# Three of the second round's low weight parts: GpSimd subtraction in place of an adding transfer

## The chip, the cores and the metric

One core of one Trainium2 chip runs the whole kernel. The metric is device time in microseconds (us) of one execution; a profiled execution gives, beside it, a trace of every engine. The engines are TensorE (PE; its weight loads PEld), VectorE (DVE), ScalarE (ACT), GpSimd (POOL) and SyncE (SP, which here only starts transfers and reads one index).

## The reference

Windowed attention is followed by a layer of eight experts. Attention: `q`, `k`, `v` are (8, 8, 576, 64); half of the heads look 32 positions back, half look at every fourth of the last 128; softmax, then times `v`. The result, as `x` of 4608 tokens by 512, goes to the experts:

```
logits = x @ w_gate                      # 4608 x 8
# tokens go to experts in the order of their logits, at most 576 to each
h = maximum(x[mask] @ w1[e], 0.0)        # w1[e]: 512 x 1024
out[mask] = h @ w2[e]                    # w2[e]: 1024 x 512
```

All is float32. Which expert fills up first, and with which tokens, depends on the data, so the kernel finds it by a search, once a round.

## The kernel before

Attention fills the first 205 us or so; the rest is `moe` (from L1110), eight rounds of one expert each. The change lies in round two, which the code counts as `r == 1`.

**A round.** A search on DVE and PE (counting matmuls, L782, between DVE steps, L796 and L819 to L832) finds the expert. `settle` and `listing` make its list of 576 tokens: `digits` on DVE, the products `rx` on POOL (`by_chunk`, L1079) and ACT, six comparisons `ob` on DVE (`within`, L1087), 18 placing matmuls (`place`, L1094), then `indices` on DVE (L1103 to L1106). Five indirect transfers on POOL (`gather`, L1258) fetch the tokens; PE turns them (L1272), and ACT and DVE split them into a high part `xh` and a low part `xl` (through one PSUM tile, so one after the other). GEMM 1 (L1309) multiplies by `w1`, GEMM 2 (L1351) by `w2`; results go out by an indirect transfer on POOL (`put`, L1377, behind a small memset, L1376) from a ring of three `y` tiles.

**Weights.** Full precision comes from two reduced parts of each float32 weight: a high one `h`, rounded by ACT, and a low one `l = raw - h`. `weights(n, r, f, deps)` (L1143) loads piece `f` of eight (128 x 512) of `w1` or `w2` (L1159, started by SP), makes `h` on ACT (`hi`, L1164, seen in the trace at the helper's line L1141), and then `l` in one of two ways. Where `(n, r)` is in `ADDED`, which holds `("2", 0)`, `("1", 1)` and `("2", 1)`, ACT writes `-h` into `l` (`ne`, L1167) and POOL starts a transfer that adds `raw` to it (L1169). Elsewhere DVE subtracts (L1171, in the trace at L1142). In round two only the first four pieces of `w1` are loaded as soon as the expert is known; the other four wait for a gate, a tiny POOL memset (L1150).

**The order of the work.** Each engine runs its instructions in the order in which they were issued, and that order is made while the program is built, by a planner (`Schedule.run`). Every piece of work has an engine, a price in ns, the pieces it needs and a boost; its due time is the length of what follows it, less the boost. On each engine the piece with the earliest due time goes next, from when it is ready; another piece goes ahead of one that is not ready yet only if it ends, by its price, at most a tolerance later than that one could start. For POOL the tolerance `TOL_POOL` is 200 ns. Some prices: `by_chunk` 750, each `within` 473, `close` (DVE) 1780, `place` 450, `indices` 620, each `get` of the gather 1250, `put` 1200, and 180 from engine to engine; the boosts are 27000 for a gather, 23000 for the list, 1500 for weights and -15000 for a `put`. In round two POOL runs, in this order: `put` of the first y tile, `rx`, the adding transfers of pieces 0, 1 and 2, `put` of the second y tile, five gathers, the gate, the adding transfer of piece 3, `put` of the third.

Of the kernel before, what the change touches and what calls it, by code (L numbers as in the profile page):

```python
# [38 lines left out]
B_L, B_G, B_T, B_X, B_H, B_HL, B_Y, B_S, B_W = 23000, 27000, 15000, 0, 20000, 17000, 28000, -15000, 1500  # L39
RAW1, D_R, NQ, AHEAD_W = 8, 262, (2, 2), (3, 4)  # L40
ADDED, T_A, T_G = (("2", 0), ("1", 1), ("2", 1)), 4500, 4500
# [114 lines left out]
class Schedule:  # L156
# [8 lines left out]
    def op(self, eng, cost, fn, deps=(), boost=0, lat=0, dma=0, buf=None):  # L165
        x = Op(len(self.ops), eng, cost, fn, deps, boost, lat, dma, buf)
        for d in x.deps:
            d.users.append(x)
        self.ops.append(x)
        return x  # L170
# [940 lines left out]
def moe(tc, ctx, C, R, xd, w1, w2, out):  # L1111
    nc = tc.nc
# [7 lines left out]
    op = K.op  # L1120
# [21 lines left out]
    sub = lambda e, o, a, b: e.tensor_tensor(o, a, b, op=OP.subtract)  # L1142
    E, gemm1_end, x_users, got, gate = {}, {}, {}, {}, {}  # L1143

    def weights(n, r, f, deps):

        raw, old, use = RAW[n].take()
        if n == "1" and r < len(AHEAD_W) and f == AHEAD_W[r]:

            gate[r] = op("POOL", 100, lambda: nc.gpsimd.memset(raw[:1, :1], 0.0), [got[r, 1], *old], B_G)  # L1150
        if r in gate:
            deps = [*deps, gate[r]]

        def load():
            if n == "1":
                src = w1[bass.ds(E[r], 1), f].rearrange("o p d f -> p (o d f)")
            else:
                src = w2[bass.ds(E[r], 1), f * 128:f * 128 + 128, :].rearrange("o p d -> p (o d)")
            nc.sync.dma_start(raw, src)  # L1159

        ld = op("SP", 60, load, [*deps, *old], dma=T_W)
        h, oldh, useh = WH[n].take()
        l, oldl, usel = WL[n].take()
        hi = op("ACT", 525, lambda: act(h, raw), [ld, *oldh], B_W)  # L1164
        if (n, r) in ADDED:
            use.append(hi)
            ne = op("ACT", 525, lambda: nc.scalar.activation(l, h.bitcast(F32), AF.Copy, scale=-1.0), [hi, *oldl], B_W)  # L1167
            useh.append(ne)
            lo = op("POOL", 1040, lambda: nc.gpsimd.dma_start(l, raw, accum_op=OP.add), [ne], B_W, lat=T_A)  # L1169
            use.append(lo)  # L1170
        else:  # L1171
            lo = op("DVE", 600, lambda: sub(nc.vector, l, raw, h), [ld, hi, *oldl], B_W)
            use += [hi, lo]
        useh.append(lo)
        return h, l, hi, lo, useh, usel
# [216 lines left out]
    def round_(r):  # L1392
        e = None
        if r:
            e = search(r) if r < NE - 1 else chain("DVE", 650, R.last, [st["fetch"], st["need"]])
        en = st["fetch"] = EN[r] = op("SP", 100, lambda: fetch(r, R.eidx), [e])
        ix, BOX[r] = settle(r, e)
        X[r] = gather(r, ix, BOX[r])
        W[r] = [weights("1", r, f, [en]) for f in range(NF)]

    round_(0)
    for r in range(NE):
        W2 = [weights("2", r, f, [EN[r]]) for f in range(NF)]
        expert(r, X[r], BOX[r], W[r], W2)
        if r + 1 < NE:
            round_(r + 1)
# [78 lines left out]
```

## Time and profile before

| what | us |
|---|---|
| median of three executions | 704.34 (703.73 to 706.86) |
| the profiled execution, its own time | 708.44 |
| its span, first to last instruction | 706.6 |

The median is of runs without a profile. Every row below comes from the one profiled execution, which took 4.10 us longer than that median, and whose span lies 1.84 us under its own time. Times in rows are us from the start of the span. A busy PE is not PE at its peak, since the ends of matmuls are modelled; spans on POOL are rough.

### The profile page before, as it was taken

Reading aid. Unit: us, or ns where it says so; the run is one execution under the profiler, and the core shown is the slowest. Engines: PE = TensorE matmul, PEld = TensorE weight load, DVE = VectorE, ACT = ScalarE, POOL = GpSimd, SP = SyncE. Lnnn points to the kernel's source line nnn. Section 1 sums busy time; section 2 is a strip of 40 time slices with the busy share of each in tenths; the row PEclk is TensorE's granted clock in tenths of the full one; section 3 lists DMA queues with packets and bytes.
Section 4 is the critical chain, followed back from the end, with each engine's and each line's share of the span. In section 5 each row is a group of like instructions: output and inputs, shape, how many; then the busy total and the mean of one; then the engine's idle time right before and its main releaser. Section 6 shows DMA issues by size and latency. Waiting matters only on the chain.

```text
span 706.6 us, 17388 instructions
## 1 busy us (share of the span) xinstructions
PE 665.0 (94%) x6579; PEld 585.0 (83%) x6581; DVE 484.7 (69%) x2086; ACT 291.4 (41%) x616; POOL 140.6 (20%) x206
## 2 busy tenths in 40 slices
PE   7899999999974899899999999999999999999995
PEld 5787899888963698699889889879978988988983
DVE  5467877789457889588689879969978854724200
ACT  3344554453521474286335434423524525424210
POOL 6111111100000332452410410310321131211011
PEclk9999999999985899999999999999999999999998
DMA  9999999973211684889314514512711574113001
GB/s 253 266 265 284 279 311 255 264 202 80 63 41 45 194 177 112 249 174 268 98 53 137 180 51 130 185 43 73 239 51 53 164 261 147 50 58 98 1 23 45
DMA packets 58524, 104.60 MB, mean 148 GB/s; under 512 B 6212, under 2 KB 27844, under 8 KB 58436
## 3 DMA queue, kind: packets, MB, share of 16 engines
q1 hardware_dynamic: 49096, 78.32, 38.7%
q0 software_dynamic: 9344, 25.17, 13.4%
q8 instruction: 51, 0.84, 0.5%
q14 instruction: 33, 0.27, 0.1%
HBM read 78.31 MB, written 18.87 MB: 138 GB/s over the span
## 4 chain that ended last, share of the span: by engine, by line
PE 68%; issue 12%; DVE 10%; POOL 3%; DMA 3%; ACT 1%; another core or an unknown queue 1%; POOLq 0%; SPq 0%; DVEq 0%
PE py L1351 18%; PE ph L1309 17%; PE pS L506 9%; PE px L514 6%; PE px L564 3%; PE pS L503 3%; PE pm L486 2%; PE ptx L1272 2%; PE pz L782 2%; PE py L1354 1%; PE py L1356 1%; POOL out L1377 1%; DVE hb L1329 1%; DVE G L796 1%; DMA qs<-in_qd 1%
## 5 line engine op out<-in xcount | busy, mean ns | idle before, releaser
L1351 PE MATMUL py<-w2h,hb 128*128 128x512 f32 x512 | 172.0, 401 | 0.0
L1309 PE MATMUL ph<-xh,w1h 128*128 128x256 f32 (+1 forms) x512 | 138.1, 300 | 0.0
L1309 PE MATMUL ph<-xl,w1h 128*128 128x256 f32 (+1 forms) x512 | 136.8, 298 | 0.0
L1309 PE MATMUL ph<-xh,w1l 128*128 128x256 f32 (+1 forms) x512 | 136.0, 296 | 0.0
L1351 PEld LDWEIGHTS py<-w2h,hb 128*128 128x128 f32 x512 | 96.7, 189 | 19.4
L1351 PE MATMUL py<-w2l,hb 128*128 128x512 f32 x256 | 100.2, 392 | 0.0
L1141 ACT ACTIVATE hb<-ph 128x256 fp32r<-128x256 f32 (+2 forms) x192 | 59.6, 345 | 88.5 <-PE ph L1309 86.9
L1309 PEld LDWEIGHTS ph<-xh,w1h 128*128 128x128 f32 x512 | 91.8, 190 | 0.5
L1309 PEld LDWEIGHTS ph<-xh,w1l 128*128 128x128 f32 x512 | 91.8, 190 | 0.1
L1309 PEld LDWEIGHTS ph<-xl,w1h 128*128 128x128 f32 x512 | 91.4, 190 | 0.1
L506 PE MATMUL pS<-q,k 128*80 128x96 f32 (+1 forms) x672 | 83.0, 265 | 0.0
L1377 POOL DMA_INDIRECT out<-y,idx x40 | 41.3, 1034 | 194.6 <-ACT y L1141 136.0
L456 ACT ACTIVATE E<-pS 96x384 f32<-96x384 f32 (+1 forms) x96 | 46.5, 486 | 75.2 <-PE pS L506 74.1
L1329 DVE SCALAR_TENSOR_TENSOR hb<-ph,hb 128x320 fp32r<-128x320 f32 (+1 forms) x128 | 57.0, 452 | 29.4 <-ACT hb L1141 25.2
L506 PEld LDWEIGHTS pS<-q,k 128*80 128x80 f32 (+1 forms) x672 | 68.5, 158 | 0.0
L1141 ACT ACTIVATE y<-py 128x512 f32<-128x512 f32 (+1 forms) x40 | 23.8, 596 | 104.0 <-PE py L1351 90.5
L493 DVE CUSTOM_DVE_ANT_0 junkm<-pm,const 128x80 bf16<-128x80 f32 (+1 forms) x336 | 59.5, 244 | 4.2 <-PE pm L486 3.6
L1351 PEld LDWEIGHTS py<-w2l,hb 128*128 128x128 f32 x256 | 48.6, 190 | 8.5
L514 PE MATMUL px<-v,E 81*64 81x65 f32 (+1 forms) x1344 | 47.9, 225 | 5.3 <-issue 2.9
L1258 POOL DMA_INDIRECT xg<-xd,idx x40 | 42.1, 1054 | 52.7 <-PE ph L1309 25.1
L514 PEld LDWEIGHTS px<-v,E 81*64 81x64 f32 (+1 forms) x1344 | 42.8, 138 | 10.2 <-issue 3.8
L1141 ACT ACTIVATE w1h<-raw 128x512 fp32r<-128x512 f32 x64 | 39.6, 628 | 27.6 <-DMA raw<-in_moe_w 27.2
(179 smaller groups left out, 1009.5 us busy)
## 6 DMA issues: line engine op xcount, KB each, us to landing
raw<-in_moe_w SPq DMA_DIRECT2D x128, 256.0 KB, 4.6
v<-in_vp SPq DMA_DIRECT2D x8, 780.0 KB, 14.2
v<-in_vd SPq DMA_DIRECT2D x8, 650.0 KB, 10.3
xd<-xs SPq DMA_DIRECT2D x16, 288.0 KB, 7.5
xd<-xs SPq DMA_DIRECT2D x32, 144.0 KB, 9.2
w2l<-raw POOLq DMA_DIRECT2D x16, 256.0 KB
qs<-in_qp SPq DMA_DIRECT2D x7, 576.0 KB, 10.1
k<-in_kp SPq DMA_DIRECT2D x7, 576.0 KB, 9.7
```

The lines of the kernel that those rows point to most:

```text
L456: e = self.op("ACT", 380, lambda j=j, pS=pS: nc.scalar.activation(self.E[:self.nk, j * self.gs:j * self.gs + self.gs], pS.tile[:, :self.gs ...
L493: nc.vector.tensor_tensor_reduce(out=jk[:, c - c0, :nk], in0=pm[:, (c - c0) * nk:(c - c0 + 1) * nk], in1=mm[:, min(1, (c if self.kind == 0 ...
L503: nc.tensor.matmul(pS[:nk, c - c0], ls[:64 + n, c], self.r[:64 + n, :2 * nq], start=(c == c0), stop=False, skip_group_check=True)
L506: nc.tensor.matmul(pS[:nk, c - c0], self.Ks[c], self.Qm[c], start=False, stop=True, skip_group_check=True)
L514: nc.tensor.matmul(px[64 * a:64 * a + 64, c - c0], lh, self.V[c][a], start=True, stop=True)
L564: nc.tensor.transpose(t[:, c], src, C["identf"])
L1141: act = lambda o, i, f=AF.Copy: nc.scalar.activation(o, i, f)
L1258: nc.gpsimd.indirect_dma_start(out=xg[:n], out_offset=None, in_=xd, in_offset=bass.IndirectOffsetOnAxis(ap=box[0][:n, m:m + 1], axis=0))
L1309: nc.tensor.matmul(o, a[:, d * 128:d * 128 + 128], b[:, d, c0:c1], start=((d, i) == pairs[0]), stop=((d, i) == pairs[-1]))
L1329: hl = op("DVE", 335 if j == 0 else 400, lambda: nc.vector.scalar_tensor_tensor(hb[:, CAP + c0:CAP + c1], o, 0.0, hb[:, c0:c1], op0=OP.max ...
L1351: nc.tensor.matmul(py, x, w, start=(f + i == 0), stop=(f == NF - 1 and i == 2))
L1377: s = nc.gpsimd.indirect_dma_start(out=out, out_offset=bass.IndirectOffsetOnAxis(ap=box[0][:n, m:m + 1], axis=0), in_=y[:n], in_offset=None)
```

## The change

For round two's `w1` (`n == "1"`, `r == 1`) and pieces 0, 1 and 2, the negated copy on ACT and the adding transfer are gone. In their place POOL subtracts, `l = raw - h`, at a price of 1900 ns, once the load and the high part are there. Pieces 3 to 7 of the same round keep the adding transfer.

```
         hi = op("ACT", 525, lambda: act(h, raw), [ld, *oldh], B_W)
-        if (n, r) in ADDED:
+        if (n, r) == ("1", 1) and f < 3:
+
+            lo = op("POOL", 1900, lambda: sub(nc.gpsimd, l, raw, h), [ld, hi, *oldl], B_W)
+            use += [hi, lo]
+        elif (n, r) in ADDED:
             use.append(hi)
             ne = op("ACT", 525, lambda: nc.scalar.activation(l, h.bitcast(F32), AF.Copy, scale=-1.0), [hi, *oldl], B_W)
             useh.append(ne)
```

`sub(e, o, a, b)` is `e.tensor_tensor(o, a, b, op=OP.subtract)`. The adding transfer that these pieces leave carried a price of 1040 and 4500 ns (`T_A`) until it lands.

## Rows read from the trace of the kernel before

**Rows 1.** From the page: the span, and the busy time of each engine with its share and its number of instructions.
```profile
span 706.6 us, 17388 instructions
...
PE 665.0 (94%) x6579; PEld 585.0 (83%) x6581; DVE 484.7 (69%) x2086; ACT 291.4 (41%) x616; POOL 140.6 (20%) x206
```

**Rows 2.** The chain of work that ended last, from 276 to 286.5 us (start, length, what).
```profile
276.00 5.47 PE py L1351 x24
281.47 0.47 PE ptx L1094 x18
281.93 4.22 PE py L1351 x18
286.15 0.56 PE pz L782 x9
```

**Rows 3.** Who waited for whom from 276 to 300 us: engine and instruction that waited, what released it, then total us, times, longest. "remote" is a release that the trace puts to no instruction.
```profile
ACT xh L1141 <- remote: 4.8, 1, 4.8
...
DVE Q L819 <- remote: 3.7, 1, 3.7
...
PE pz L782 <- DVE G L796: 2.7, 1, 2.7
...
PE ptx L1272 <- DVE xl L1142: 0.5, 1, 0.5
```

**Rows 4.** The same core by stretches: length, busy us and instructions (x) of PE, PEld, DVE, ACT and POOL, then the granted TensorE clock as a share of full speed, the DMA engines' busy share, GB/s.
```profile
292.00:294.80 2.80, 0.14 (x2) 0.07 (x2) 1.98 (x9) 0.60 (x1) 0.26 (x1) 1.00 1.03 245
294.80:298.50 3.70, 3.23 (x18) 2.71 (x18) 3.32 (x12) 1.12 (x2) 0.00 (x0) 0.54 1.04 384
```

**Rows 5.** GpSimd (POOL) in order of time, 277 to 291 us: start, length, engine, line, operation, names, and in brackets the idle time before it and what ended that.
```profile
277.62 1.04 POOL L1079 TENSOR_TENSOR rx<-oa,const 128x360 bf16<-128x360 bf16 x1 [0.75 <-DVE oa L1074]
278.61 0.88 POOL L1169 DMA_DIRECT2D w1l<-raw  x1
...
282.50 1.04 POOL L1377 DMA_INDIRECT out<-y,idx  x1 [0.28 <-issue]
283.84 1.03 POOL L1258 DMA_INDIRECT xg<-xd,idx  x1 [0.30 <-DVE A L1053]
...
289.86 0.09 POOL L1150 MEMSET raw<- 1x1 f32 x1
289.89 1.03 POOL L1169 DMA_DIRECT2D w1l<-raw  x1
```

**Rows 6.** ScalarE (ACT) in order of time, columns as in rows 5: the first round-two weight pieces, and the copy out of the round-one matmul result that comes last.
```profile
276.66 0.63 ACT L1141 ACTIVATE w1h<-raw 128x512 fp32r<-128x512 f32 x1 [1.13 <-DMA raw<-in_moe_w]
277.33 0.63 ACT L1167 ACTIVATE w1l<-w1h 128x512 fp32r<-128x512 f32 x1
...
278.35 0.62 ACT L1141 ACTIVATE w1h<-raw 128x512 fp32r<-128x512 f32 x1
...
303.60 0.59 ACT L1141 ACTIVATE y<-py 64x512 f32<-64x512 f32 x1
```

**Rows 7.** Grouped rows: line, engine, operation, names, shape, number | busy us, mean ns of one | idle before, and what ended it. GpSimd's issuing of the eight adding transfers into w1l, and VectorE's subtractions into w1l in the other rounds, both over the whole span; then VectorE's wider hb subtractions from 300 to 620 us.
```profile
L1169 POOL DMA_DIRECT2D w1l<-raw x8 | 7.5, 940 | 9.5 <-ACT w1h L1141 8.5 <-ACT w1l L1167 1.0
...
L1142 DVE TENSOR_TENSOR w1l<-raw,w1h 128x512 fp32r<-128x512 f32 x56 | 36.2, 684 | 0.1
...
L1329 DVE SCALAR_TENSOR_TENSOR hb<-ph,hb 128x320 fp32r<-128x320 f32 x48 | 23.3, 486 | 8.1 <-ACT hb L1141 4.8 <-issue 2.8
```

**Rows 8.** VectorE (DVE) against GpSimd, columns as in rows 5. The six ob instructions of round two together; its second and its fourth alone; then rx on GpSimd and the ob beside it in a later round; then rx on GpSimd and an hb subtraction, which reads PSUM, beside it.
```profile
277.45 3.50 DVE L1087 TENSOR_TENSOR ob<-si,const 128x384 bf16<-128x384 int32 x6
...
277.92 1.16 DVE L1087 TENSOR_TENSOR ob<-si,const 128x384 bf16<-128x384 int32 x1
...
279.47 0.55 DVE L1087 TENSOR_TENSOR ob<-si,const 128x384 bf16<-128x384 int32 x1
...
381.66 0.79 POOL L1079 TENSOR_TENSOR rx<-oa,const 128x360 bf16<-128x360 bf16 x1 [14.27 <-DVE oa L1074]
...
381.89 0.97 DVE L1087 TENSOR_TENSOR ob<-si,const 128x384 bf16<-128x384 int32 x1
...
326.84 0.79 POOL L1079 TENSOR_TENSOR rx<-oa,const 128x360 bf16<-128x360 bf16 x1 [2.51 <-DVE oa L1074]
...
327.03 0.49 DVE L1329 SCALAR_TENSOR_TENSOR hb<-ph,hb 128x320 fp32r<-128x320 f32 x1 [0.27 <-ACT hb L1141]
```

**Rows 9.** TensorE (PE) in order of time: the list's placing matmuls, the first count of the next search, and the first turn of a gathered tile.
```profile
281.31 0.62 PE L1094 MATMUL ptx<-rx,ob 128*128 128x40 bf16 x18
...
286.00 0.46 PE L782 MATMUL pz<-G,ohr 128*128 128x64 bf16 x9
...
289.41 0.63 PE L1272 MATMUL ptx<-const,xg 128*128 128x128 f32 x4
```

**Rows 10.** Stretches with idle TensorE and the ones behind them, columns as in rows 4.
```profile
18.40:20.70 2.30, 0.00 (x0) 0.00 (x0) 1.12 (x5) 1.06 (x2) 0.00 (x0) 1.00 1.01 204
...
22.00:25.40 3.40, 3.40 (x29) 3.24 (x26) 2.36 (x26) 0.49 (x1) 0.00 (x0) 0.50 1.04 383
...
58.60:59.90 1.30, 0.05 (x2) 0.05 (x2) 0.51 (x1) 0.00 (x0) 0.00 (x0) 1.00 1.02 357
...
59.90:63.00 3.10, 3.10 (x50) 2.88 (x50) 2.33 (x20) 0.55 (x2) 0.74 (x2) 1.00 1.04 387
```

## The prediction

> **What bounds the kernel now.** I read the page first. PE is busy 665.0 of 706.6 us and POOL 140.6 [rows 1], so a change on POOL matters only where it moves a wait of PE. Then the chain of waits around the change: from 276 to 286.5 us it is PE alone, back to back, with the placing matmuls of the token list and the first count of the next search among the GEMM's [rows 2]. So in this stretch nothing can be won by relieving ACT, POOL or the transfers, and whatever holds PE's next instruction is lost in full, because the later rounds are PE's too.
>
> The view of who waited for whom shows the one hole nearby: PE waits 2.7 us for VectorE's G and 0.5 for xl [rows 3]. Behind that wait stand VectorE and ACT, both held 3.7 and 4.8 us by a release that the trace puts to no instruction. The table by stages shows PE nearly empty from 292 to 294.8, then granted 0.54 of its clock for 3.7 us [rows 4], mostly the lower of its two levels, 1.2 GHz. The hole costs 2.7 + 0.5 + 3.7 x 0.46 = 4.9 us. The profiled execution took 708.44; without the hole it would have been 703.5, close to the median of the runs shown, 704.34, and to the fastest, 703.73. So I read the hole as belonging to this execution, not to the median, and say below what follows if that is wrong.
>
> **What is removed.** Three negated copies on ACT, 0.63 us each [rows 6]: 1.9 us of ACT, whose own wait there is for loads (1.13 us before the first w1h). Nothing on PE waits for them; I cost this at nothing, covered by PE's GEMM 2. Three issues on POOL at 0.94 [rows 7], 2.8 us, and three transfers. These could have delayed the gathers behind them on the same queue. But the first gathered tile, issued at 283.84 [rows 5], is turned by PE at 289.41 with no wait noted [rows 9]. So no gain is taken; its bounds are 0 and the whole hole, 4.9, should the transfers be what held VectorE and ACT.
>
> **What is added, and where the planner puts it.** By the prices in the code, rx ends 0.93 us after the list's digits; two subtractions at 1.90 end at 4.73. The indices are ready at 5.24 (six within at 0.473, close 1.78, indices 0.62) and the gathers can start at 5.42. A third subtraction would end at 6.63, past 5.42 plus the tolerance of 0.20. So subtractions 0 and 1 run between rx and the gathers. The second y tile's put, a 1.20 piece that may start only when its tile is copied, no longer fits either. Behind the gathers the gate and piece 3 come by due time, then subtraction 2, then the two puts. Moving that put by some 12 us costs nothing: its tile is next written at 303.60 [rows 6]. SP's loads for pieces 4 to 7 wait for the gate, a POOL memset that stays behind the five gathers and slides with them.
>
> **Price of a subtraction on POOL.** The trace has none of this kind. The nearest POOL row with two SBUF inputs is rx, 0.79 us for 360 columns where it does not wait [rows 8]; scaled to 512, 1.12. The low bound is VectorE's own subtraction of this shape, 0.684 [rows 7]; the high one is rx as it ran in round two, 1.04 [rows 5], scaled: 1.48. I take 1.12, because the engine and the kind of work are the same. GPSIMD Engine Reference in the Trainium skill (Engine selection) puts a two-input operation on GpSimd at about twice VectorE's time, which would be 1.37; the sum below would then be 0.5 us higher, an estimate by that page that nothing here needs.
>
> **What it blocks.** This is the step that decides. After rx, VectorE runs the list's six ob comparisons, 3.50 us in all, ending at 280.95; PE's placing matmuls start at 281.31 [rows 8, 9]. That is a margin of 0.36. An ob takes 0.55, but 1.16 beside rx in round two and 0.97 in a later round, where it ends 0.41 us after rx ends (382.86 against 382.45) [rows 8]. So VectorE does nothing of an ob while rx runs, and then does it whole. The first two high parts are ready early (276.66 + 0.63, and 278.35 + 0.62 [rows 6]), so subtractions 0 and 1 run directly behind rx, among the five ob that remain. VectorE loses both: 2 x 1.12 = 2.24 us. PE's stall is 2.24 - 0.36 = 1.9 us. With the bounds on the price it is 1.0 to 2.6; with all three ahead of the gathers it is 3.0. The rest of VectorE's work (the indices, G, the count that PE reaches at 286.00) slides by the same 2.2, as PE has by 1.9, so it is not paid twice; the gathers start about 2.2 later too, and their tiles keep their lead on PE.
>
> The third subtraction, near 293 to 295 us, meets a search step and the xl subtractions. Those read PSUM, and an hb subtraction of that kind took 0.49 beside rx [rows 8], against a mean of 0.486 [rows 7]. So only a step that reads two SBUF tiles can be held. Bounds 0 and 1.12; I take 0.3, near the low end because of the hb row. SBUF — State Buffer in the Trainium skill (Who interferes with whom) says the same split as a rule: a VectorE instruction with two SBUF inputs waits for the whole of a GpSimd instruction that reads SBUF, one with a single SBUF input not at all. The trace agrees (0.97 against 0.55 for ob, 0.49 against 0.486 for hb). Were it sharing instead, each subtraction would cost what rx cost the ob of round two, 0.61 us, scaled 0.87, and the stall would be 1.4 instead of 1.9.
>
> **The sum.** 1.9 + 0.3 = 2.2 us more. On the profiled execution's own time that is 710.6 with its hole, 705.7 without. On the median, which I take to have no hole, it is 704.34 + 2.2 = **706.5**.
>
> **Rivals.** First, slower: the stall lowers PE's clock. An idle stretch of 2.3 us in attention was followed by 3.4 us at half clock, one of 1.3 us by none [rows 10]; the forecast's 1.9 lies between. Half of 3.4 us is 1.7, giving 708.2. It decides at an idle time somewhere from 1.3 to 2.3 us. For it: the hole above also ended at the low clock [rows 4]. Against it: with the low price the stall is 1.0, under the stall that did nothing.
>
> Second, faster: the hole is in the timed runs as well, and the three transfers make it, since they run on the queue just ahead of it. Then 4.9 goes and 2.2 comes: 701.6; with the subtractions hidden, 699.4. For it: the hole follows the only stretch where adding transfers and gathers share a queue. Against it: the unexplained release, the first gather's timely landing, and 708.44 against 704.34.
>
> Third, nothing happens: subtractions wait behind the gathers, or POOL takes its turn only where VectorE reads one SBUF tile. Then nothing on PE moves and the time is 704.3. Against it: the prices place two of them ahead, and rx got its turn among the ob.
>
> **How the numbers follow.** About 0.5% (3.5 us) is what a measurement of this kernel can tell from no change; the bounds are 700.8 and 707.9. Forecast 0.45, with stalls of 1.0 to 3.0 plus 0 to 1.1: 705.3 to 708.4, a tenth of it over the bound. Clock 0.25, most of it over the bound. Nothing 0.14. Hole 0.16, half of it under 700.8. Slower 0.04 + 0.22 = 0.26, faster 0.08, same 0.66. The range reaches from 701.5, which takes in the hole with the subtractions paid, to 709.0, which takes in the clock with a stall somewhat longer than forecast; what it leaves out is half of the hole's chance and the tail of the clock's.
>
> **What the profile after would show.** Right: two POOL subtractions of 1.0 to 1.5 us between rx and the first gather; two of the ob at 1.5 us or more, or one near 2.8; PE idle close to 2 us ahead of the placing matmuls, put to VectorE; the first gather 2 us later against the list's digits. Wrong: PE without a gap there (then VectorE was not held, or the planner put the work elsewhere); a subtraction of 1.9 us or longer, which makes the stall 3.4; a hole near 292 that is gone from timed runs too, told by a median near 701; a granted clock of 0.5 behind the stall, which is the first rival.

## The result

Twelve executions of each kernel: a median of 709.21 us (705.20 to 715.17) after, 704.28 (701.14 to 708.93) before; ratio 1.0076, 95% interval 1.0051 to 1.0101, which is 3.6 to 7.1 us more. A second series of the changed kernel, of six executions, gave 1.0100 (1.0070 to 1.0129). The forecast was 706.5, 2.2 us more than before, in a range from 701.5 to 709.0. The sign was the forecast's; the median lies 2.7 us above the forecast and 0.2 above the range, and the stages below account for 6.1 us instead of 2.2.

### The profile page after: what moved, and what is told of

It reads as the page before. It is cut to its first block, busy times and chain, and to the rows that moved or that the text cites. A ratio compares the mean times of both kernels' runs of the same rounds, so it can differ in the third digit from the quotient of the medians.

```text
span 711.3 us, 17384 instructions
## 1 busy us (share of the span) xinstructions
PE 666.4 (94%) x6581; PEld 585.3 (82%) x6581; DVE 489.0 (69%) x2086; ACT 289.6 (41%) x613; POOL 142.7 (20%) x206
## 4 chain that ended last, share of the span: by engine, by line
PE 66%; DVE 13%; issue 12%; POOL 3%; DMA 3%; ACT 1%; SPq 0%; POOLq 0%; DVEq 0%
PE ph L1313 17%; PE py L1355 16%; PE pS L506 9%; PE px L514 6%; PE pS L503 3%; PE px L564 3%; PE pm L486 2%; DVE ob L1087 2%; PE ptx L1276 2%; PE pz L782 2%; DVE hb L1333 1%; PE py L1358 1%; PE py L1360 1%; DMA raw<-in_moe_w 1%; DVE G L796 1%
```

## The profile after

From the page, as in [rows 1]; this execution, one of the twelve, took 713.04 us, 3.8 over the median:

```profile
span 711.3 us, 17384 instructions
...
PE 666.4 (94%) x6581; PEld 585.3 (82%) x6581; DVE 489.0 (69%) x2086; ACT 289.6 (41%) x613; POOL 142.7 (20%) x206
```

ACT has lost 1.8 us of work (1.9 were counted); VectorE, which got no new instruction, is busy 4.3 us longer. GpSimd in order of time, against [rows 5] (start, length, engine, line, operation, names, idle before and what ended it):

```profile
280.63 1.04 POOL L1079 TENSOR_TENSOR rx<-oa,const 128x360 bf16<-128x360 bf16 x1 [0.75 <-DVE oa L1074]
281.64 3.17 POOL L1142 TENSOR_TENSOR w1l<-raw,w1h 128x512 fp32r<-128x512 f32 x2
288.94 1.06 POOL L1262 DMA_INDIRECT xg<-xd,idx  x1 [4.14 <-DVE A L1053]
...
295.55 0.09 POOL L1150 MEMSET raw<- 1x1 f32 x1
295.58 1.02 POOL L1173 DMA_DIRECT2D w1l<-raw  x1
296.23 1.68 POOL L1142 TENSOR_TENSOR w1l<-raw,w1h 128x512 fp32r<-128x512 f32 x1
297.45 0.45 POOL L1380 MEMSET spacer<- 1x1 f32 x1
298.11 1.36 POOL L1381 DMA_INDIRECT out<-y,idx  x1 [0.20 <-issue]
```

The order is the forecast's to the instruction: two subtractions behind rx, five gathers, gate, piece 3, the third subtraction, puts. VectorE's ob and G, against [rows 8], same columns:

```profile
280.46 5.70 DVE L1087 TENSOR_TENSOR ob<-si,const 128x384 bf16<-128x384 int32 x6
...
282.00 3.22 DVE L1087 TENSOR_TENSOR ob<-si,const 128x384 bf16<-128x384 int32 x2
...
292.68 0.82 DVE L796 SCALAR_TENSOR_TENSOR G<-V,delta,const 128x576 bf16<-128x576 f32 x1
295.84 2.69 DVE L796 SCALAR_TENSOR_TENSOR G<-V,delta,kb 128x576 bf16<-128x576 f32 x1
```

Two of the six ob took 1.6 us each instead of 0.55; one G took 2.69 instead of 0.82, the one beside the third subtraction. The chain of work that ended last, against [rows 2] (start, length, what), is no longer PE's alone:

```profile
280.54 5.62 DVE ob L1087 x6
...
289.20 0.47 DVE oh L893
...
289.70 1.17 ACT ohr L906
290.87 0.05 issue
290.92 0.46 PE pz L782 x9
```

TensorE's own rows, against [rows 3, 9]: the placing matmuls, the first count of the next search, then the count for which TensorE waits 1.51 us, and the turn of a gathered tile behind that.

```profile
284.29 0.40 PE L1094 MATMUL ptx<-rx,ob 128*128 128x40 bf16 x9
285.28 0.24 PE L1094 MATMUL ptx<-rx,ob 128*128 128x40 bf16 x3 [0.60 <-DVE ob L1087]
285.75 0.24 PE L1094 MATMUL ptx<-rx,ob 128*128 128x40 bf16 x3 [0.22 <-DVE ob L1087]
286.21 0.24 PE L1094 MATMUL ptx<-rx,ob 128*128 128x40 bf16 x3 [0.23 <-DVE ob L1087]
290.92 0.46 PE L782 MATMUL pz<-G,ohr 128*128 128x64 bf16 x9 [0.28 <-ACT ohr L906]
...
298.58 0.45 PE L782 MATMUL pz<-G,ohr 128*128 128x64 bf16 x9 [1.51 <-DVE G L796]
299.52 0.66 PE L1276 MATMUL ptx<-const,xg 128*128 128x128 f32 x4 [0.49 <-DVE xl L1142]
```

So there are two stalls, where the forecast had one of this size. In the first the eighteen placing matmuls spread over 2.16 us (284.29 to 286.45) instead of 0.62, with 1.05 us of idle time between them and 0.28 ahead of the count; in the second TensorE is idle for 1.51 and 0.49. What each costs is read from the stage lengths below: some 1.9 us. The stretches behind the second, columns as in [rows 4], show no drop of the clock:

```profile
297.00:298.60 1.60, 0.09 (x2) 0.02 (x2) 1.60 (x2) 0.00 (x0) 1.40 (x3) 1.00 0.90 262
298.60:302.00 3.40, 2.91 (x22) 2.39 (x22) 3.19 (x12) 1.51 (x3) 1.94 (x3) 1.00 1.07 313
```

The third difference stands at the very end. The view of line 1485, the end of the program, lists GpSimd's three DRAIN instructions, which are not counted as busy time: name, count, shortest/median/longest in ns, first and last start.

```profile
L1485 POOLq DRAIN  x3: 46/107/9532, 700.9 to 711.0; - x3
```

The kernel before, in its third profile (below), at its line 1481:

```profile
L1481 POOLq DRAIN  x3: 46/107/7257, 696.2 to 704.0; - x3
```

The long drain begins 0.7 us behind the end of the last matmul. It took 9.53 us instead of 7.26, and the span ends some 0.8 us behind it.

The table is worked out from the starts of matmuls. A: first GEMM 2 matmul of round one to first GEMM 1 matmul of round two, the stage of the change. B: from there to round two's first GEMM 2 matmul. End: last matmul to the end of the span. Drain: the long one.

| kernel | A | B | end | drain | ratio (95%) |
|---|---|---|---|---|---|
| before, as first shown | 35.51 | 28.84 | 8.79 | 7.26 | |
| e1 before again | 31.29 | 32.44 | 8.80 | 7.26 | 1.0009 (0.998 to 1.0037) |
| e11 before, third | 31.81 | 29.30 | 8.79 | 7.26 | 1.0008 (0.9975 to 1.0041) |
| after | 35.05 | 29.27 | 11.07 | 9.53 | 1.0076 (1.0051 to 1.0101) |
| e5 after again | 35.04 | 30.31 | 11.07 | 9.53 | 1.0100 (1.0070 to 1.0129) |
| e2 two by GpSimd | 33.14 | 33.83 | 8.89 | 7.16 | 1.0085 (1.0057 to 1.0112) |
| e12 the same again | 33.33 | 33.03 | 8.89 | 7.17 | 1.0031 (0.9999 to 1.0064) |
| e7 one by GpSimd | 32.18 | 29.19 | 8.74 | 7.21 | 1.0034 (1.0005 to 1.0063) |
| e3 fills, no reads | 31.33 | 29.11 | 11.07 | 9.53 | 1.0043 (1.0012 to 1.0074) |
| e4 nothing in place | 31.24 | 29.21 | 11.07 | 9.53 | 1.0027 (0.9998 to 1.0057) |
| e10 three by VectorE | 33.97 | 31.63 | 11.07 | 9.54 | 1.0006 (0.9974 to 1.0039) |

Ahead of A lie attention and round one's start, which none of these edits touches but which took 264.5 to 272.2 us in these profiles; from round two's GEMM 2 to round seven's it is 284.6 to 285.9 us in every row, and 78.9 from there to the last matmul. One kernel's ratio also differs from series to series, which this scatter may explain; no run shows that it does. End and drain repeat to a few hundredths. A repeats where no long wait or drop of the clock of its own falls into it: 31.0 to 31.8 in six profiles without a GpSimd subtraction (e1, e3, e4, e11, e15, e18), 35.0 to 35.1 in seven with three. The exceptions are the first profile of the kernel before (35.51), e10 (33.97), e16 (36.65) and e17 (35.41).

## The experiments: who holds VectorE

Theory: a GpSimd subtraction that reads SBUF holds a VectorE instruction that reads two SBUF tiles. Rivals: what is removed costs or gains; or chance.

**e1_before_again**, **e5_after_again** and **e11_before_third**: no edit.

> The kernel before, unchanged, for a second profile of it. If the hole near 292 us of the first profile belongs to that execution alone, the placing matmuls, the counts and the turns of round two come without a PE gap over 0.5 us, and the stage from the first GEMM 2 matmul of round one to the first GEMM 1 matmul of round two takes 30.6 us (35.5 less 4.9). If the hole is the kernel's own, it is there again and the stage takes 35 us. The ratio to the kernel before is 1.000 either way and shows the spread.

> The changed kernel once more, for a second profile. Blocking theory: the six list comparisons (ob) again take 5.7 us instead of 3.5 and G 2.7 instead of 0.8, and the stretch from the first GEMM 2 of round one to the first GEMM 1 of round two is again near 35.1 us (31.3 in the two kernels that had no GpSimd subtractions). End theory: GpSimd's last instruction, the drain of its queue, again takes 9.5 us, not the 7.26 of the kernel before, and the time from the last matmul to the end is 11.1 against 8.8. If instead the long drain was a chance of those profiles, it comes out at 7.2 here. Time: 1.0076 of the kernel before, 1.005 to 1.010.

> The kernel before once more, for a third profile of it. Its two profiles had the stretch of two stages (first GEMM 2 of round one to first GEMM 2 of round two) at 64.35 and 63.73 us, each with one wait that the other did not have; the kernels without subtractions had 60.45. If those waits are rare, this profile has 60.5 to 61.5, and the changed kernel's 64 is 3.5 us more, which with the drain's 2.3 is more than the 4.9 that was measured; if they are the rule, it is near 64 again and the changed kernel gets back in the second stage what it lost in the first. Time ratio 1.000.

The hole of [rows 3] came back in neither repeat of the kernel before: A is 31.3 and 31.8, so the hole cost 3.7 to 4.2 us and not the 4.9 of the prediction. The changed kernel repeated itself: A 35.04, ob 5.70, G 2.73, drain 9.53. In B e1 had a 2.7 us wait that e11 did not have, so such waits come and go in the kernel before; A and B of e11 are 61.1 together, as was expected if they are rare.

**e2_two** and **e12_two_again**: the third piece back to its transfer.

```
-        if (n, r) == ("1", 1) and f < 3:
+        if (n, r) == ("1", 1) and f < 2:
```

> Pieces 0 and 1 by GpSimd's subtraction, piece 2 by the adding transfer again. Blocking theory (VectorE stands still while a GpSimd subtraction reads its two tiles): ob takes 5.7 us for six and PE loses 1.9 us there, as in the changed kernel, but the count step behind the gathers runs undisturbed, its G at 0.82 us and not 2.69, which gives back the 2.0 us lost there: about 707 us, ratio 1.004. Rival (the later gathers and puts, or GpSimd's time, cost the 4.9 us): nothing comes back, ratio 1.007.

> Two pieces by GpSimd once more. First time: first stage 33.14 us, second stage 33.83 (29.3 in the changed kernel), with PE waiting 2.7 us for a search step of VectorE that stood behind a hidden copy of ACT, that behind a load, that behind an adding transfer; ratio 1.0085. If that is the rule (two transfers and the puts crowd the software queue behind the gathers), the second stage is again 33 to 34 us and the ratio 1.007 to 1.009. If it was a chance of that execution, the second stage is near 29.3 and the ratio near 1.003.

A is 33.14 and 33.33: the first two subtractions cost 1.8 to 2.0 over 31.3, and the third another 1.7 to 1.9, to 35.05. G is 0.82 again. But what A gave back, B took: TensorE waited 2.7 us there in both profiles, as it had in e1 (e12: instruction that waited, releaser, total us, times, longest), and in e12 ScalarE had stood 5.2 us for a load ahead of it:

```profile
PE pz L1028 <- DVE ge L991: 2.7, 1, 2.7
```

```profile
311.75 0.63 ACT L1141 ACTIVATE w2h<-raw 128x512 fp32r<-128x512 f32 x1 [5.22 <-DMA raw<-in_moe_w]
```

With pieces 2 and 3 both added by transfer behind the gathers, two puts follow on the same queue, and the loads of the second weights wait for buffers that adding transfers free. That chain is read from the trace, not tested, and since e1 has the same wait without these subtractions, that the order of e2 brings it about is not shown. The ratios, 1.0085 and 1.0031, agree with each other only as scatter; the theory had 1.004.

**e7_one**: `f < 1`.

> Only piece 0 by GpSimd's subtraction, pieces 1 and 2 by adding transfers as before: 103 transfers on the software queue. Blocking theory: one subtraction among the ob comparisons, which take 3.5 + 1.1 = 4.6 us; PE's wait for the placing is 1.1 - 0.36 = 0.75; no subtraction meets G (0.82). The stretch is 31.3 + 0.75 = 32.1 us. Drain: by the number, a third value that no run has shown yet (104 and 102 gave 7.26 and 7.16, 101 gave 9.53): 7.2 if only the third transfer crosses a limit, 9.5 if odd numbers take the longer one; by bytes 7.2. Time with the short drain and without loss elsewhere 1.001, with the long one 1.004; if the transfers that stay lose time in round two's GEMM 1, as they did with two subtractions, up to 1.007.

ob took 4.71 in all, A is 32.18, 0.9 over 31.3 (0.75 expected), G 0.82, and the drain 7.21. No rise in B. With two subtractions A rises by 1.9, with one by 0.9, where VectorE lost 2.2 and 1.2: beyond the margin of 0.36, what VectorE loses there is lost to PE, each time.

**e3_memset**: GpSimd writes zeros into the low part twice, instead of subtracting; the low parts of three pieces are left out.

```
-            lo = op("POOL", 1900, lambda: sub(nc.gpsimd, l, raw, h), ...)
+            def fill_():
+                for _ in range(2):
+                    nc.gpsimd.memset(l.bitcast(F32), 0.0)
+            lo = op("POOL", 1900, fill_, ...)
```

> In place of each subtraction GpSimd writes zeros twice over the same 128x512 tile, so it works about as long in the same places but reads no SBUF; the low parts of the three pieces are left out. Blocking theory with the read side shared: ob stays at 3.5 us for six, G at 0.82, no PE gap at the placing matmuls, ratio 1.000. If the write side is shared as well, ob and G are as long as in the changed kernel and the ratio is 1.005 to 1.008. Rival (time on GpSimd and later gathers and puts): ratio 1.005 to 1.008 with ob at 3.5 us.

GpSimd and VectorE in e3, same columns as above:

```profile
281.93 2.16 POOL L1169 MEMSET w1l<- 128x512 f32 x4
...
293.74 1.55 POOL L1169 MEMSET w1l<- 128x512 f32 x2
```

```profile
280.77 3.50 DVE L1087 TENSOR_TENSOR ob<-si,const 128x384 bf16<-128x384 int32 x6
...
294.19 0.82 DVE L796 SCALAR_TENSOR_TENSOR G<-V,delta,kb 128x576 bf16<-128x576 f32 x1
```

The fills lie on the ob and on G, and neither grows; A is 31.33. So neither GpSimd's being busy nor its writing holds VectorE; of what the subtraction does beyond that, reading SBUF is what the theory names. SBUF — State Buffer in the Trainium skill (Who interferes with whom) says that a VectorE instruction with two SBUF inputs contends with a GpSimd instruction that reads SBUF, and not with one that only writes it; the trace agrees (0.82 beside a fill, 2.69 beside a subtraction).

**e4_none**: copy, transfer and subtraction all gone, the low parts of three pieces being those left there by round one.

```
-            lo = op("POOL", 1900, lambda: sub(nc.gpsimd, l, raw, h), [ld, hi, *oldl], B_W)
-            use += [hi, lo]
+            lo = hi
+            use.append(hi)
```

> The three negated copies and adding transfers are taken out and nothing is put in their place; the low parts of these three pieces are those of round one's weights, so they are left out of the result. It prices the removal alone. Forecast: nothing on PE waits for them, ratio 1.000, ob at 3.5 us, gathers at most 1 us earlier against the digits. Rival (the transfers make the hole, also in timed runs): ratio 0.993, and no hole in the profile.

A is 31.24: what was removed neither costs nor gains in the stage. And yet neither e3 nor e4 is faster than before (1.0043 and 1.0027, the second with an interval that just reaches 1; 1.000 was expected of both), though A and B are about as short as any: both have the long drain.

**e10_dve3**: the three subtractions on VectorE (`op("DVE", 600, lambda: sub(nc.vector, l, raw, h), ...)`).

> The same three pieces without a transfer, but subtracted by VectorE instead of GpSimd; the planner puts two right behind the ob comparisons and one behind a count's G. Blocking theory: nothing of GpSimd's runs beside VectorE, ob takes 3.5 us and every G 0.82; VectorE itself spends 3 x 0.68 = 2.05 us, of which the two behind ob lie beside PE's GEMM 2, so the stretch is 31.3 to 32.0 us against 35.05; the drain stays long (8,912 packets, 9.53 us). Time: 2.3 + 0 to 0.7 over the kernel before, 1.003 to 1.004. Rival: what cost the time is that three subtractions are done at all at that place, by whichever engine; then the stretch is 33.4 us or more and the ratio 1.006 to 1.01.

ob is 3.50 and every G 0.82, as the theory has it. But A came out at 33.97, where the rival had put it: one wait of 1.3 us for a G that VectorE began late, and a granted clock of 0.53 over 3.4 us behind it. e15 (below), with the same order, had A at 31.03 without either. The ratio, 1.0006, lies under what either side expected (1.003 and 1.006). So the price of three VectorE subtractions in A is left open by these two; that nothing was held is clear.

## The experiments: the long drain

**e6_pad3**, **e8_pad1**, **e9_pad5**: the changed kernel with three, one, five software transfers of one element at the start of attention.

```
+    ... pad = R.pf.tile([1, 8], F32, name="pad"); [op("POOL", 1000, lambda i=i: nc.gpsimd.dma_start(pad[:, i:i + 1], T["in_cf"][:1, i:i + 1]), (), B_P) for i in range(3)]
```

> The changed kernel with three more transfers on GpSimd's software queue, of one element each, at the start of attention: 104 transfers on that queue in the whole program, as in the kernel before (101 in the changed one). Theory: the length of the last drain goes by the number of transfers that the queue has carried, so it comes back to 7.26 us, the rest behind the last matmul to 8.8, and the kernel takes 2.3 us less than the changed one: 1.0043 of the kernel before, with the blocking (35.1 us in the stretch) untouched. Rival: the drain goes by the bytes or by what sort of transfer the queue carried; three of four bytes change nothing, the drain stays at 9.5 and the ratio at 1.0076.

> The changed kernel with one more software transfer of one element at the start of attention: 102 on the queue, as in the kernel with two subtractions. By the number the last drain takes 7.16 us as there; by bytes or kind 9.5. Nothing else in the trace should differ from the changed kernel: ob 5.7, G 2.7 us.

> The changed kernel with five software transfers of one element at the start of attention, 9,072 packets on that queue in all. So far the last drain took 9.53, 9.61 and 9.77 us at 8,912, 8,944 and 9,008 packets, and 7.16, 7.21 and 7.26 at 9,056, 9,200 and 9,344, so it is not the number of transfers. Theory: it goes by the packets that the queue has carried, with a step between 9,008 and 9,056; five tiny transfers cross it, the drain takes 7.2 us and the kernel 2.3 us less than the changed one (ratio near 1.005). Rival: it goes by the bytes or by the adding transfers themselves; then the drain grows on along the line of the tiny ones, to 9.9 us, and the ratio stays near 1.008 to 1.010. In both the stretch from GEMM 2 of round one to GEMM 1 of round two stays at 35.05 us.

Drains of 9.77, 9.61 and 9.93 us, where the theories had 7.2: it goes neither by the number of transfers (104 in e6, as before) nor by the packets (e9 has 9,072 and the long drain, e2 9,056 and the short one); each tiny transfer adds 0.08 us. Ratios of 1.011 (1.008 to 1.014) and 1.0051 (1.0017 to 1.0086) for three and five; A at 35.04 to 35.07 in all. e8, like e14, e16, e17 and e18 below, is a single execution, so that only its trace counts.

**e13_big1**, **e14_col1**, **e15_dve3_big1**: one plain transfer of 128 rows of 2 KB, one of 128 rows of 4 bytes, and the first of these in the VectorE version.

> The changed kernel with one software transfer of 128 rows of 2 KB (256 KB, a plain copy, nothing added) at the start of attention. Tiny transfers did not shorten the last drain (9.53 us, 9.93 with five), whatever their number and packets; the three runs with one more adding transfer or more had 7.16 to 7.26. Theory: the drain goes by what the queue has carried in rows or bytes; one such transfer brings it back to 7.2 us, the end behind the last matmul to 8.8, and takes 2.3 us off the changed kernel (ratio near 1.005 where the changed one has 1.0076 and 1.010). Rival: it is the adding transfers into w1l that matter, by their kind or their place in round two; then the plain copy leaves it at 9.5 to 9.7.

> The changed kernel with one software transfer of 128 rows of one element (512 bytes) at the start of attention. If the drain goes by rows (descriptors), it is 7.2 us, as with the 256 KB one; if by bytes, it stays at 9.5 to 9.7. If it goes by neither, both stay long.

> Three pieces by VectorE and one 256 KB software transfer in attention: no GpSimd subtraction beside VectorE, three adding transfers fewer, and, if the theory of the rows holds, the short drain. It is the version that might beat both: VectorE's version had a ratio of 1.0006 with the long drain, so 1.0006 - 2.3/706 = 0.997 with the short one, the stretch near 31.5 to 34 us. If the drain stays long: 1.0006 again.

9.61 us in all three: neither rows nor bytes (e13 moved 24.65 MB on that queue, as e2 did). e13:

```profile
L1485 POOLq DRAIN  x3: 51/103/9607, 702.9 to 713.0; - x3
```

The ratios are 1.012 (1.0064 to 1.0175) for e13 and 1.0064 (1.0034 to 1.0095) for e15. The version that was to beat both kernels is not faster than the kernel before. It is e10 but for one transfer in attention, and e10 had 1.0006: so far apart come out two series of nearly one program, and a single ratio settles less than its interval says.

**e16_add1**, **e17_late3**, **e18_w2three**: the changed kernel with one adding transfer at the start of attention, into a tile that nothing reads; the changed kernel with a tiny plain transfer behind each subtraction; and the kernel before with three other adding transfers gone (second weights of round two, `("2", 1)`, pieces 0 to 2, subtracted by VectorE; the text below says round one of them).

```
+    ... nc.gpsimd.memset(pad, 0.0), nc.gpsimd.dma_start(pad, T["in_moe_w1"][0, 0]..., accum_op=OP.add) ...
```

```
+            ... sub(nc.gpsimd, l, raw, h), nc.gpsimd.dma_start(LATE[:, f:f + 1], w1[0, 0, :1, 0, :1]) ...
```

```
-        if (n, r) in ADDED:
+        if (n, r) in ADDED and not ((n, r) == ("2", 1) and f < 3):
```

> The changed kernel with one adding transfer of 256 KB at the start of attention, into a tile that nothing uses: 22 adding transfers in all, as in the kernel with two subtractions (24 before, 21 after). If the last drain goes by the number of adding transfers, wherever they stand, it is 7.2 us; if by their place in round two, 9.6 as with the plain copy.

> The changed kernel with a plain software transfer of one element behind each of the three subtractions: 104 transfers on the queue, the three at the place of those removed. If the drain goes by the number of transfers behind some point of the program (place), it is 7.3 us; if adding is what counts, 9.7. The blocking stays: ob 5.7 us.

> The kernel before with three other adding transfers gone: pieces 0 to 2 of round one's second weights by VectorE's subtraction, the first weights of round two untouched. 21 adding transfers and 101 in all, as in the changed kernel. If the number of adding transfers or of all decides, the drain is 9.5 us; if the place of the changed kernel's three, 7.2.

e16, then e18:

```profile
L1485 POOLq DRAIN  x3: 51/103/7162, 695.6 to 703.3; - x3
```

```profile
L1481 POOLq DRAIN  x3: 46/107/9532, 697.0 to 707.0; - x3
```

One adding transfer in attention, far ahead of the change and without any use, takes 2.4 us off the drain (9.53 to 7.16); three fewer at another place make the kernel before end like the changed one. Tiny transfers at the place of the three (e17) leave it long, 9.78. So it is the number of adding transfers: 24, 23 and 22 gave 7.26, 7.21 and 7.16, 21 gave 9.53 in five kernels. Why a drain asks for that, why between 22 and 21, and what fewer than 21 would do, stays open. No DMA engine is busy in its last 4 us, before or after.

e17 shows what sets the price of the third subtraction, since the transfers shifted it against G. GpSimd's subtraction and VectorE's G, columns as above:

```profile
295.97 1.71 POOL L1142 TENSOR_TENSOR w1l<-raw,w1h 128x512 fp32r<-128x512 f32 x1
```

```profile
296.76 1.53 DVE L796 SCALAR_TENSOR_TENSOR G<-V,delta,kb 128x576 bf16<-128x576 f32 x1
```

Here G began 0.8 us behind the subtraction; in the profile after, G is noted as begun 0.4 ahead of it (295.84 against 296.23). In both G ended 0.6 us behind the subtraction's end. So G stood until the subtraction was through, and the later it came, the less it lost: 0.71 us in e17 instead of 1.87, and TensorE waited 0.36 for it instead of 1.51.

e16 also shows the clock. Behind the same wait for G, the stretches (columns as in [rows 4]) are:

```profile
290.50:292.80 2.30, 0.45 (x9) 0.32 (x8) 2.27 (x5) 0.00 (x0) 2.10 (x3) 1.00 0.96 261
292.90:296.30 3.40, 3.38 (x10) 2.89 (x11) 2.46 (x10) 1.12 (x2) 1.02 (x2) 0.50 1.02 328
```

A is 36.65 there, 1.6 over the changed kernel's. PE waited 1.57 us in e16 and 1.51 in the profile after, where the clock stayed at 1.00, as it did behind the same wait in six more profiles (1.51 to 1.55). In e17 it fell to 0.50 for 3.4 us behind the first stall, among the placing matmuls (idle 0.89, 0.23 and 0.22 us), and A is 35.41 there, although the third subtraction cost less.

## Why the prediction was wrong, point by point

- **The hole** belongs to that execution: right. Two further profiles of the kernel before have none there. Its price was 3.7 to 4.2 us (35.51 against 31.81 and 31.29), not 4.9.
- **The place of the subtractions**: right, each one. The first gather started 8.3 us behind rx instead of 6.2, later by the 2 us that were forecast.
- **The price, 1.12 us**: right for what the ob lose, not for what the trace writes. The pair took 3.17 us on GpSimd, 1.6 each, outside the 1.0 to 1.5 that the text looked for and short of its "1.9 or longer". But ob grew from 3.50 to 5.70, 1.1 for each: by starts and ends, the noted span begins some 0.45 us before the ob ahead of it ends. So a span beside VectorE isn't the time lost. By the text's rival of sharing, 0.87 each, ob would have grown to 5.24.
- **The first stall, 1.9 us**: right. A is 1.8 to 2.0 longer than 31.3 with two (e2, e12; 1.3 to 2.3 over the whole spread of 31.0 to 31.8), 0.9 with one (e7).
- **The third subtraction, 0.3**: the first step that failed. It cost 1.7 to 1.9 (35.05 against 33.14 and 33.33), six times the term and over its upper bound of 1.12. The text named a search step and the xl subtractions, took them to read PSUM, and chose a value near the hb row. What the subtraction met was a G, which reads its two tiles from SBUF, as the ob do; the step of the search that matters was not looked up. G was held by 1.87 us, and TensorE counts with that G next, without a margin: 1.51 at the count and 0.49 at the turn. By the starts and ends, it lost 1.87 where an ob lost 1.1 because it stood through the whole noted span of 1.68 (e17, where it came later, lost 0.71); why that span is 1.68 with no ob beside it is open.
- **The removal, "cost at nothing"**: the second step that failed. Its bounds were 0 and a gain; a loss was not bounded. In A it is nothing (31.24 and 31.33 in e4 and e3), but at the end of the program it is 2.3 us, by the drain, which the runs tie to the number of adding transfers. No row had been read there: the end is no part of the stage, and the drain is no instruction that counts as busy.
- **The sum**: 1.9 + 1.9 + 2.3 = 6.1 us instead of 2.2, ratio 1.0087; measured 1.0076 and 1.0100. Without subtractions 2.3 us, 1.0033, against 1.0043 (e3) and 1.0027 (e4). With the short drain and one subtraction 0.9, 1.0013, inside e7's interval. It does not fit everywhere: two subtractions would give 1.0027, inside e12's interval and well under e2's, whose B is longer; and e9's interval ends at 1.0086, under the 1.0092 that its drain would give.
- **Rivals**: the clock did not fall in the profile after, but it did in e16, behind a like wait, for the 1.6 us that the rival had put at 1.7, and in e17. So it falls in some executions, and idle time alone, by which the text had it decide, does not: 1.31 us in e10 was followed by the low level, 1.55 in e8 was not. That the transfers make the hole in every execution is false (e1, e11, and e4, which lacks them and is no faster); what made it in the one execution that has it is not shown. That nothing happens is false.

## What to carry to other kernels

Here GpSimd work that reads SBUF was paid by VectorE where VectorE read two SBUF tiles (1.1 us of an ob, up to 1.9 of a G). So look up the operands of what runs beside each moved piece, and count it in full where TensorE waits for VectorE next. Read the end of the program too: there the number of transfers of a kind showed, far from the change. Compare stage lengths between profiles where the scatter of whole executions hides the sum.

## What the hardware showed that was not expected

GpSimd's last drain is 2.3 us longer with 21 adding transfers in the program than with 22, 23 or 24, in each of the three places tried, and each plain transfer more adds 0.08 us to the long one (9.61, 9.77 and 9.93 with one, three and five). A write by GpSimd held VectorE by nothing (G 0.82 beside it), a subtraction that reads by up to 1.9 us, and a G that was noted as begun 0.4 us ahead of that subtraction was held by it all the same. And the same wait of 1.5 us was followed by full clock in seven executions and by 3.4 us at 0.50 in another.
